# First DFT stage of batches 3 to 7: from one product over 94 rows to GpSimd sums and differences of mirrored rows and two products over 120 rows

## The chip, the cores and the metric

The kernel runs on one NeuronCore of a Trainium2 chip. Its engines have queues of their own and meet at semaphores: TensorE (PE, matmul), VectorE (DVE), ScalarE (ACT), GpSimd (POOL) and SyncE (SP, which here only issues DMAs). GpSimd issues DMAs too, in the same queue as its arithmetic, one instruction after the other. The metric is the time of one execution on the device in microseconds; the median of the runs of the kernel before is 788.53 us.

## The reference, cut to what matters

```python
# x (8, 3008, 256), filt_r and filt_i (1505, 256), w_in (256, 2048), w_out (2048, 256), alpha (2048)
X = np.fft.rfft(x, axis=1)
y = np.fft.irfft(X * (filt_r + 1j * filt_i), n=3008, axis=1)      # global filter along the sequence
h = y.reshape(24064, 256) @ w_in
g = h + np.sin(alpha * h) ** 2 / alpha
out = g @ w_out                                                   # float32
```

The two dense products with the snake activation between them are most of the arithmetic. The change touches only the first step of the forward transform.

## The kernel before, in words

The length 3008 is 47 * 64. A row n of a batch is 64 * n1 + n2, with n1 from 0 to 46 and n2 from 0 to 63. The transform of one batch (class `Spectral`) has four stages:

- `first` (L178, product in L181): a DFT of length 47 over n1, for 24 frequencies s, real and imaginary part. An x tile holds 94 partitions (47 n1, and for each the two halves of n2) and 8 columns n2 of 256 channels. One product of 94x96 weights with 512 columns makes two of these 8. There are 16 products for each batch. `evac` (L155 to L162) copies each result from PSUM to the tile `t1_h` in fp16, in turn two on ACT (L160) and one on DVE (L162). After every fourth, one DMA on SP writes 8 columns to a buffer `d1` in DRAM (L186).
- `load_t2` (L193): eight DMAs on POOL read `d1` back with n2 on the partitions.
- `forward`, `product`, `cross`, `inverse` (u from 0 to 11): a DFT over n2 on PE (L201), a copy on ACT (L204), a swap of its halves by DMA (L208), three DVE operations of two SBUF operands each (`product` L215, `cross` L221 and L222) that multiply with the filter, and the inverse product on PE (L232).
- `load_t4` and `last`: back through DRAM, and the inverse over n1 into the tile `y` (L254).

The dense part works on chunks of 512 columns of `y`. `hidden` (L540) makes one of 16 blocks of 128 hidden units with two products into one of 4 PSUM buffers (pool `hps`). ACT computes a cosine of it (L544), and a DVE SCALAR_TENSOR_TENSOR reads the cosine from SBUF and the block from PSUM and writes `v` (L545). The PSUM buffer is free when this DVE operation is done. `project` (L557) makes the output from the `v` of the chunk before.

The order is written by hand. A loop counts steps, eight to a chunk: a step issues two `hidden`, one or two pieces of transform work from a sorted list, a part of `project`, and more transform work. `put(at, ...)` gives each piece the step where it is due. Batch b has z = 48 * b, and its pieces are due relative to z, so the transform of batch b runs beside the dense part of the batches before. Work of PE is let out at one piece for each half step, other work when it is due. This sets the order of each engine's queue; when an instruction runs depends on that order and on its semaphores alone. For batches 3 to 7 the dues were: x loads at z - 92 + 7 * ch, the 16 `first` at z - 67 + 0.66 * i, `load_t2` at z - 56, `forward` at z - 46.8 + 2.3 * u, `product` 1.5 and `cross` 4.5 later, `inverse` at z - 40.8 + 2.3 * u. An x load (L141) also waits for the latest L545 that was issued before it, so it starts close to its due step.

Of the kernel before, what the change touches and what calls it, by code (L numbers as in the profile page):

```python
# [9 lines left out]
FP16 = mybir.dt.float16  # L10
FP32 = mybir.dt.float32
BF16 = mybir.dt.bfloat16
UINT32 = mybir.dt.uint32
AFT = mybir.ActivationFunctionType
ALU = mybir.AluOpType
# [3 lines left out]
B, S, C = 8, 3008, 256  # L19
DFF = 2048  # L20
N1, N2 = 47, 64
NS, NQ = 24, 64
NR = 2 * N1
NK = 4 * NS
FUSED = 1


def dft_tables():

    n1, n2 = np.arange(N1), np.arange(N2)  # L30
    s, q = np.arange(NS), np.arange(NQ)
    ph = 2 * np.pi * np.outer(n1, s) / N1
    w = np.stack([np.cos(ph), -np.sin(ph)], 1)
    wf = np.zeros((N1, 2, 2, NS, 2))
    wi = np.zeros((2, NS, 2, N1, 2))
    v = np.stack([2 * np.cos(ph), -2 * np.sin(ph)], 0)
    v[0, :, 0], v[1, :, 0] = 1.0, 0.0
    for h in range(2):
        wf[:, h, :, :, h] = w
        wi[:, :, h, :, h] = v.transpose(0, 2, 1) * (8.0 / S)  # L40

    kap = np.where(q[:, None] < 32, s + N1 * q[:, None], s + N1 * (95 - q[:, None]))
    sg = np.where(q < 32, 1.0, -1.0)[:, None]
    th = 2 * np.pi * n2[:, None, None] * kap / S
    c, sn = np.cos(th), np.sin(th)
    d = np.zeros((2, N2, NS, 2, NQ))
    d[0, :, :, 0] = c.transpose(0, 2, 1)
    d[1, :, :, 0] = sn.transpose(0, 2, 1)
    d[0, :, :, 1] = (-sn * sg).transpose(0, 2, 1)
    d[1, :, :, 1] = (c * sg).transpose(0, 2, 1)  # L50
    f16 = np.float16
    wf, wi = wf.reshape(N1 * 2, 2, NS, 2), 2 * wi.reshape(2, NS, 2, NR)
    wf0, wi0 = np.zeros((96, 2, 2, 32)), np.zeros((2, 2, 32, NR))
    wf0[:NR, :, :, :NS] = wf.transpose(0, 1, 3, 2)
    wi0[:, :, :NS] = wi.transpose(0, 2, 1, 3)
    d = d.reshape(128, NS, 128).astype(f16)
    e = d.transpose(2, 1, 0) * f16(0.125)
    return (wf.reshape(NR, NK).astype(f16), wi.reshape(NK, NR).astype(f16), d,
            wf0.reshape(96, 128).astype(f16), wi0.reshape(128, NR).astype(f16), e)


# [1 line left out]
def kernel(  # L63
# [8 lines left out]
    out: bass.AP,  # L72
):
    nc = tc.nc
    wf_host, wi_host, d_host, wf0_host, wi0_host, e_host = dft_tables()
    wf_dram = nc.inline_tensor(wf_host, name="wf_tbl")
    wi_dram = nc.inline_tensor(wi_host, name="wi_tbl")
    d_dram = nc.inline_tensor(d_host, name="d_tbl")
    wf0_dram = nc.inline_tensor(wf0_host, name="wf0_tbl")
    wi0_dram = nc.inline_tensor(wi0_host, name="wi0_tbl")  # L80
# [6 lines left out]
    def after(ins, other):  # L87

        tc.add_manual_dep(ins.ins, other.ins.name, mybir.DependencyInfo(
            mybir.DependencyClass.Sync, mybir.DependencyReason.DATA), reason="order of loads")  # L90

    def pool(name, bufs, space=None):
        kw = {} if space is None else {"space": space}
        return ctx.enter_context(tc.tile_pool(name=name, bufs=bufs, **kw))

    cpool = pool("consts", 1)
    xpool = pool("xp", 4)
    t2pool = pool("t2", 4)
    xfpool = pool("xf", 3)
    ppool = pool("pp", 4)  # L100
# [4 lines left out]
    dpool = pool("dram", 2, DRAM)  # L105
    fps = pool("fps", 2, PSUM)
# [1 line left out]
    ops = pool("ops", 2, PSUM)  # L108

    wf_t = cpool.tile([NR, NK], FP16)  # L110
    t1_h = [cpool.tile([128, 16, C], FP16, name=f"t1_h{i}") for i in range(2)]
    t4_a = cpool.tile([128, 2, 16, C], FP16)
    t4_h = [t4_a[:, i] for i in range(2)]

    def by_half(t):

        return t.rearrange("p a (b c) -> p (a b) c", c=128)

    cos_all = cpool.tile([128, 4, 512], FP32)
    y = cpool.tile([128, 2, 2, 32, NR], FP16)  # L120
# [4 lines left out]
    for h in range(2):  # L125
        nc.sync.dma_start(out=x32[:, 4 * C * h:4 * C * h + 4 * C],
                          in_=bass.AP(tensor=x.tensor, offset=x.offset + 4 * h * C, ap=[[32 * C, 96], [1, 4 * C]]))
# [8 lines left out]
    marks = {}  # L136

    def load_x(b, ch):
        xt = xpool.tile([NR, 8, C], FP16, name=f"x_{b}_{ch}", tag="x")
        for n0, n in [(0, 8)] if b or ch < 3 else [(0, 4), (4, 4)]:  # L140
            ins = nc.gpsimd.dma_start(  # L141
                out=xt[:, n0:n0 + n],
                in_=bass.AP(tensor=x.tensor, offset=x.offset + (b * S + ch * 8 + n0) * C,
                            ap=[[32 * C, NR], [C, n], [1, C]]),
            )
        if b == 0:
            marks["x", ch] = ins
        if b == 1:
            marks["x1", ch] = ins
            after(ins, marks["w_out"])  # L150
        if b > 1:
            after(ins, marks["snake"])
        return xt
# [3 lines left out]
    def evac(dst, src, on_act=None):  # L157
        flip[0] = (flip[0] + 1) % 3
        if flip[0] if on_act is None else on_act:
            marks["act"] = nc.scalar.copy(out=dst, in_=src)  # L160
        else:
            marks["dve"] = nc.vector.tensor_copy(out=dst, in_=src)  # L162

    class Spectral:

        def __init__(self, b):
            self.b = b
            self.d1 = dpool.tile([2 * NS, N2, C], FP16, name=f"d1_{b}", tag="d1")
            self.d2 = dpool.tile([2 * NS, N2, C], FP16, name=f"d2_{b}", tag="d2")
            self.d1_rows = self.d1.rearrange("a (h n) c -> (a h) n c", h=2)  # L170
            self.d2_rows = self.d2.rearrange("a (h n) c -> (a h) n c", h=2)
            self.x, self.t2, self.t4, self.xf, self.xs, self.p = {}, {}, {}, {}, {}, {}
            self.fused = b >= FUSED

        def load_x(self, ch):
# [2 lines left out]
        def first(self, i):  # L178
            ch, j = divmod(i, 4)
            ps = fps.tile([128, 512], FP32, name=f"pa_{self.b}_{i}", tag="f")  # L180
            marks["pe"] = nc.tensor.matmul(out=ps[0:NK, :], lhsT=wf_t, rhs=self.x[ch][:, 2 * j:2 * j + 2, :],  # L181
                                           start=True, stop=True)
            r0 = 8 * (ch % 2)
            evac(t1_h[ch // 2][0:NK, r0 + 2 * j:r0 + 2 * j + 2, :], ps[0:NK, :])
            if j == 3:
                nc.sync.dma_start(out=self.d1_rows[:, 8 * ch:8 * ch + 8, :],   # L186
                                  in_=t1_h[ch // 2][0:NK, r0:r0 + 8, :])

        def load_t2(self, g):
            self.t2[g] = t2pool.tile([128, 6, C], FP16, name=f"t2_{self.b}_{g}", tag="t2")  # L190
# [73 lines left out]
    id32 = cpool.tile([16, 16], FP32)  # L264
    nc.scalar.dma_start(out=id32, in_=id32_dram.ap())

    x0 = [xpool.tile([NR, 8, C], FP16, name="x_0_0", tag="x")] + [load_x(0, ch) for ch in range(1, 4)]
    nc.gpsimd.dma_start(out=d_t, in_=d_dram.ap())
    id16 = cpool.tile([128, 128], FP16)
    nc.gpsimd.dma_start(out=id16, in_=id16_dram.ap())  # L270
# [25 lines left out]
    for g in range(2):  # L296
        gs = slice(12 * g, 12 * g + 12)
        for k, filt in enumerate((filt_r, filt_i)):
            for q in range(2):
                if (g, k, q) == (0, 1, 1):  # L300
# [3 lines left out]
                    out=f_t[k][64 * k + 32 * q:64 * k + 32 * q + 32, gs, :],  # L304
# [132 lines left out]

    def product_0(i):
        hc, w = blocks[i]
        p0[i] = xpool.tile([128, 2, 4, 128], FP16, name=f"p_0_{i}", tag="x")  # L440
        marks["products"] = nc.vector.tensor_tensor(
            out=p0[i].rearrange("p f s (k c) -> p f s k c", k=2),
            in0=xf0[i].rearrange("p s (k c) -> p s k c", k=2)[:, None].to_broadcast([128, 2, 4, 2, 64]),
            in1=filt_t[:, :, 4 * w:4 * w + 4].rearrange("p f s (k c) -> p f s k c", k=2)[..., 64 * hc:64 * hc + 64],
            op=ALU.mult)
# [24 lines left out]
            after(ins, marks["filt", 1, 1])  # L470
    nc.sync.dma_start(out=wf_t, in_=wf_dram.ap())
    nc.sync.dma_start(out=wi_t, in_=wi_dram.ap())
    w_out32 = vpool.tile([128, 16, C], FP32, name="w_out32", tag="v")
    for jb in range(0, 16, 8):
        ins = nc.sync.dma_start(out=w_out32[:, jb:jb + 8],
# [117 lines left out]
    def put(at, fn, *args, pe=False):  # L593
        pending.append((at, len(pending), pe, fn, args))
# [14 lines left out]
    for b in range(1, B):  # L609
        s = s1 if b == 1 else Spectral(b)  # L610
        z = 48 * b
        if b > 1:
            for ch in range(4):
                put((22,27,32,37)[ch] if b == 2 else z - 92 + 7 * ch, s.load_x, ch)
        for i in range(16):
            put(7.9 + 0.3 * i if b == 1 else 36 + 0.66 * i if b == 2 else z - 67 + 0.66 * i, s.first, i, pe=True)
        for g in range(4):
            put(12.5 if b == 1 else max(z - 56, 46.5), s.load_t2, g)
        for u in range(12):
            inv = 23.5 + 1.25 * u if b == 1 else 59 + 2.1 * u if b == 2 else z - 40.8 + 2.3 * u  # L620
            fwd = inv - (6 if b == 1 else 6)
            put(fwd, s.forward, u, pe=True)
            put(fwd + (0.5 if b == 1 else 1.5), s.product, u)
            if s.fused:
                put(fwd + (4 if b == 1 else 4.5), s.cross, u)
            put(inv, s.inverse, u, pe=True)
        for ch in range(4):
            put(z - (9.5 if b == 1 and ch < 3 else (10.5, 10.5, 10.5, 3)[ch]), s.load_t4, ch)
        for u in range(16):
            put(z + (u - (5 if b == 1 else 6.5) if u < 4 else 2 * u - 9), s.last, u, pe=True)  # L630
# [59 lines left out]
```

## Time and profile before

| | |
|---|---|
| runs before | 787.25, 788.53, 788.79 us; median 788.53 us |
| profiled execution, first to last instruction (span) | 786.7 us |
| median of the runs less that span | 1.8 us |
| PE / DVE / ACT / POOL busy | 773.5 / 657.6 / 616.5 / 79.5 us |
| granted TensorE clock | 1.000 |
| L181, the first-stage products of batches 1 to 7 | 112 |
| L215, L221, L222, the filter's DVE operations | 84 each |
| x loads on POOL, L141: POOL time of one, time to landing | 0.54 us, 4.9 us |
| loads of `d1`, L193: POOL time of one, time to landing | 0.67 us, 4.6 us |

The profile has no time of its own for the profiled execution beyond the span; the 1.8 us are what the runs show around it. Busy time of PE is the union of its matmuls. Because they overlap in the pipeline, the mean of one (0.38 us for 512 columns) is longer than what one adds to the end. The chain of work that ended last shows what each added.

### The profile page before, as it was taken

The page shows a single profiled execution, that of the slowest core. Times are in us where ns is not written, and L with a number is a line of the kernel's source. Part 1 is how long each engine was busy: PE and PEld are TensorE (multiplying, and loading weights), DVE is VectorE, ACT ScalarE, POOL GpSimd, SP SyncE. Part 2 cuts the span into 40 slices and gives each one's busy share as a digit, 9 for nine tenths or more (in the row PEclk, how much of TensorE's full clock was granted, in tenths as well). Part 3 has the DMA queues.
Part 4 walks back from the last instruction along what each step waited for, and adds up shares of the span by engine and source line. Part 5 has one row for each costly group of instructions (what it writes and reads, how often), then busy time and mean ns, then how long its engine had stood idle before and what let it go on. Part 6 is the DMA issues. An engine that isn't in the chain of part 4 may idle for free.

```text
span 786.7 us, 16619 instructions
## 1 busy us (share of the span) xinstructions
PE 773.5 (98%) x5799; PEld 535.0 (68%) x5799; DVE 657.6 (84%) x1172; ACT 616.5 (78%) x1208; POOL 79.5 (10%) x125
## 2 busy tenths in 40 slices
PE   8998999999999999999999999999999999999998
PEld 4756766666667766777666766777666776766666
DVE  7887997899878997799977998799987999777773
ACT  5797878888878887888877888788887887777674
POOL 6442000200020000200020000200002000000000
PEclk9999999999999999999999999999999999999999
DMA  9965568665473646554575454845556243421111
GB/s 213 258 131 157 113 145 223 153 123 133 134 198 84 134 99 195 143 120 110 120 200 128 103 106 139 224 87 113 129 155 181 61 99 81 117 62 28 41 41 54
DMA packets 87692, 100.99 MB, mean 128 GB/s; under 512 B 14488, under 2 KB 75944, under 8 KB 87608
## 3 DMA queue, kind: packets, MB, share of 16 engines
q1 hardware_dynamic: 78032, 73.73, 34.5%
q0 software_dynamic: 9360, 26.15, 17.7%
q8 instruction: 45, 0.74, 0.4%
q14 instruction: 39, 0.32, 0.1%
q10 hardware_dynamic: 216, 0.05, 0.0%
HBM read 55.72 MB, written 46.66 MB: 130 GB/s over the span
## 4 chain that ended last, share of the span: by engine, by line
PE 89%; DVE 5%; ACT 2%; DMA 2%; issue 1%; SPq 1%; ACTq 0%; DVEq 0%
PE po L557 39%; PE ph L540 38%; PE pa L181 3%; PE pd L254 2%; DVE v L545 2%; PE pb L201 2%; PE pc L232 2%; DMA xs<-xf 1%; ACT cos_all L544 1%; DMA al<-in_moe_alpha_dram 1%; PE warm L381 1%; PE pc L453 0%; SPq L585 0%; ACT t_h L160 0%; DVE filt_t L162 0%
## 5 line engine op out<-in xcount | busy, mean ns | idle before, releaser
L545 DVE SCALAR_TENSOR_TENSOR v<-cos_all,ph 128x512 f16<-128x512 f32 (+1 forms) x768 | 483.0, 672 | 108.1 <-ACT cos_all L544 104.8
L544 ACT ACTIVATE cos_all<-ph 128x512 f32<-128x512 f32 (+1 forms) x768 | 411.1, 592 | 93.9 <-PE ph L540 92.9
L540 PE MATMUL ph<-y,w 128*128 128x512 f16 (+1 forms) x1536 | 388.4, 374 | 1.7 <-DVE y L162 0.9
L557 PE MATMUL po<-w,v 128*128 128x256 f16 x3008 | 389.5, 272 | 0.0
L557 PEld LDWEIGHTS <-v 128*128 128x128 f16 x3008 | 288.3, 98 | 77.7 <-issue 1.4
L540 PEld LDWEIGHTS <-w 128*128 128x128 f16 x1536 | 147.9, 98 | 106.5 <-issue 6.1
L565 ACT COPY o<-po 128x512 f32<-128x512 f32 (+1 forms) x97 | 55.6, 574 | 20.2 <-PE po L557 12.9
L204 ACT CAST xf<-pb 128x512 f16<-128x512 f32 x84 | 50.0, 595 | 16.4 <-PE pb L201 12.7
L193 POOL DMA_DIRECT2D t<-d x56 | 36.4, 669 | 204.6 <-DMA out_dram<-o 99.8
L160 ACT CAST t_h<-pa 96x512 f16<-96x512 f32 x74 | 43.3, 585 | 10.6 <-PE pa L181 10.5
L141 POOL DMA_DIRECT2D x<-in_x_dram x32 | 17.1, 536 | 298.2 <-PE pc L232 171.2
L160 ACT CAST y<-pd 128x376 f16<-128x376 f32 (+1 forms) x82 | 39.5, 482 | 8.8 <-PE pd L254 5.3
L254 PEld LDWEIGHTS <-t_a 96*128 96x128 f16 x448 | 31.3, 97 | 18.7 <-issue 0.4
L181 PE MATMUL pa<-x,wf_t 94*96 94x512 f16 x112 | 42.3, 381 | 1.6 <-ACT t_h L160 1.3
L160 ACT CAST g<-pc 128x512 f16<-128x512 f32 x58 | 34.4, 593 | 8.0 <-PE pc L232 7.7
L222 DVE TENSOR_TENSOR p<-p,xs 128x512 f16<-128x512 f16 x84 | 35.7, 425 | 2.9
L254 PE MATMUL pd<-wi_t,t_a 96*128 96x94 f16 x448 | 37.1, 204 | 0.0
L221 DVE TENSOR_TENSOR xs<-xs,filt_t 128x512 f16<-128x512 f16 x84 | 35.2, 420 | 0.8 <-DMA xs<-xf 0.8
L215 DVE TENSOR_TENSOR p<-xf,filt_t 128x512 f16<-128x512 f16 x84 | 35.2, 419 | 0.0
L232 PE MATMUL pc<-p,e_t 128*128 128x256 f16 x168 | 32.1, 273 | 0.8 <-ACT xf L204 0.5
L201 PE MATMUL pb<-t,d_t 128*128 128x256 f16 x168 | 32.1, 272 | 0.2
L162 DVE CAST y<-pd 128x376 f16<-128x376 f32 (+2 forms) x46 | 24.9, 544 | 1.5 <-PE pd L343 1.0
(66 smaller groups left out, 264.4 us busy)
## 6 DMA issues: line engine op xcount, KB each, us to landing
x<-in_x_dram POOLq DMA_DIRECT2D x30, 376.0 KB, 4.9
d<-t_h SPq DMA_DIRECT2D x28, 384.0 KB
t<-d POOLq DMA_DIRECT2D x56, 192.0 KB, 4.6
xs<-xf SPq DMA_DIRECT2D x168, 64.0 KB
d<-g SPq DMA_DIRECT2D x56, 192.0 KB
t_a<-d SPq DMA_DIRECT2D x28, 384.0 KB
out_dram<-o SPq DMA_DIRECT2D x104, 80.0 KB
w_out<-in_moe_w_out_dram SPq DMA_DIRECT2D x2, 1024.0 KB
```

The lines of the kernel that those rows point to most:

```text
L160: marks["act"] = nc.scalar.copy(out=dst, in_=src)
L181: marks["pe"] = nc.tensor.matmul(out=ps[0:NK, :], lhsT=wf_t, rhs=self.x[ch][:, 2 * j:2 * j + 2, :], start=True, stop=True)
L193: nc.gpsimd.dma_start(out=self.t2[g][64 * p:64 * p + 64, :, :], in_=self.d1[a0:a0 + 6, :, :].rearrange("s n c -> n s c"))
L201: nc.tensor.matmul(out=ps[:, i, :], lhsT=d_t[:, s, :], rhs=self.t2[s // 6][:, s % 6, :], start=True, stop=True)
L204: nc.scalar.copy(out=self.xf[u], in_=ps)
L232: nc.tensor.matmul(out=ps[:, i, :], lhsT=e_t[:, 2 * w + i, :], rhs=pt[:, i, :], start=(k == 0), stop=(k == len(pr) - 1))
L254: nc.tensor.matmul(out=psv[:, i, :], rhs=wi_t, start=True, stop=True, lhsT=t4_h[ch // 2][0:NK, n0 % 16 + i, cb * 128:cb * 128 + 128])
L540: nc.tensor.matmul(out=ps[:, 0:n], lhsT=w1[:, cb, jb * 128:jb * 128 + 128], rhs=y_cols[:, cb, c0:c0 + n], start=(cb == 0), stop=(cb == 1))
L544: nc.scalar.activation(out=cs[:, 0:n], in_=ps[:, 0:n], func=AFT.Sin, bias=float(np.pi / 2))
L545: marks["snake"] = nc.vector.scalar_tensor_tensor(out=v[k][:, jb, 0:n], in0=cs[:, 0:n], scalar=-1.0, in1=ps[:, 0:n], op0=ALU.add, op1=ALU. ...
L557: nc.tensor.matmul(out=pso[k][:, t % 2, :], lhsT=v[k][:, jb, 128 * t:128 * t + 128], rhs=w2[:, jb, :], start=(jb == 0), stop=(jb == 15))
L565: nc.scalar.copy(out=o[:, i0:t % 2 + 1, :], in_=pso[k][:, i0:t % 2 + 1, :])
```

## The change

For a real input, the cosine is even and the sine odd in n1, so rows n1 and 47 - n1 can be added and subtracted first. Batches 3 to 7 (`FOLDED = 3`) do this on GpSimd:

- A batch's 64 columns n2, and one of padding ahead of them, are cut into 5 groups (j) of 13 (l). `mirror[0]` holds the rows n1 = 1 to 23 for the 5 groups on 115 partitions, and the five groups of row 0 on 5 more; `mirror[1]` holds rows 46 down to 24, and zeros on the last 5 (cleared once, `start_folding`). They lie in the four x slots, which are now one tile `x_all`.
- `load_mirror` loads pairs of columns l: 14 DMAs and one for row 0, in place of 4, all on POOL. They are due at z - 92 to z - 75.1.
- `fold(i)`, i from 0 to 6: one GpSimd addition of 120x512 into one of 4 small buffers `sums`, and one subtraction in place (120x256 for i = 6). In POOL's queue they come after the batch's loads and ahead of its `load_t2`.
- `first_folded(i, k)`: one product of 120x120 with 512 columns for the sums (k = 0, real part) and one for the differences (k = 1, imaginary part); with 256 columns for i = 6. 14 products and 13 copies in place of 16 and 16.
- `d1` is written by two pairs of DMAs on SP, after i = 3 and i = 6. `load_t2` is due at z - 53 instead of z - 56.

A table `wp_t` is loaded at the start, on SP, ahead of `w_out`. Batches 0 to 2 compute as before.

```diff
-    xpool = pool("xp", 4)
-    t1_h = [cpool.tile([128, 16, C], FP16, name=f"t1_h{i}") for i in range(2)]
+    t1_a = cpool.tile([128, 2, 16, C], FP16)
+    t1_h = [t1_a[:, i] for i in range(2)]
+    wp_t = cpool.tile([NF, 2, NF], FP16)
+    x_all = cpool.tile([128, 4, 8, C], FP16)
...
+    STORES = {3: 0, 6: 8}
+    NP = (NL + 1) // 2
+    x_rows = x_all.rearrange("p a n c -> p (a n) c")
+    mirror = [x_rows[:, 16 * k:16 * k + NL, :] for k in range(2)]
+    sums = [t[0:NF, NL:NL + 2, :] for t in (t1_h[0], t1_h[1], x_rows[:, 0:16], x_rows[:, 16:32])]
+
+    def start_folding():
+        nc.gpsimd.memset(mirror[1].bitcast(UINT32), 0)
...
+        def load_mirror(self, k, l0, n):
+            rows = [mirror[k][0:NF - NJ, l0:l0 + n]] + ([] if k or l0 else [mirror[k][NF - NJ:NF]])
+            for at, t in zip((N2 * (N1 - 1) if k else N2, 0), rows):
+                run = n if at else NL
+                ins = nc.gpsimd.dma_start(
+                    out=t, in_=bass.AP(tensor=x.tensor, offset=x.offset + (self.b * S + at - 1 + l0) * C,
+                                       ap=[[NL * C, NJ], [-N2 * C if k else N2 * C, NS - 1 if at else 1],
+                                           [1, run * C]]))
+                after(ins, marks["snake"])
+
+        def fold(self, i):
+            l0, n = 2 * i, min(2, NL - 2 * i)
+            xa, xb = [t[0:NF, l0:l0 + n, :] for t in mirror]
+            self.e[i] = sums[i % 4]
+            nc.gpsimd.tensor_tensor(out=self.e[i][:, 0:n, :], in0=xa, in1=xb, op=ALU.add)
+            nc.gpsimd.tensor_tensor(out=xa, in0=xa, in1=xb, op=ALU.subtract)
+
+        def first_folded(self, i, k):
...
+            nc.tensor.matmul(out=dst, lhsT=wp_t[:, k, :], rhs=src, start=True, stop=True)
+            if n == 2:
+                evac(t1_a[0:NF, k, l0:l0 + 2, :], ps[0:NF])
+            elif k == 1:
+                evac(t1_a[0:NF, :, l0, :], ps[0:NF])
+            if i in STORES and k == 1:
+                lo = STORES[i]
+                n = l0 + n - lo
+                for part in range(2):
+                    nc.sync.dma_start(out=self.d1_fold[part, :, lo:lo + n, :], in_=t1_a[0:NF, part, lo:lo + n, :])
...
-        if b > 1:
-            for ch in range(4):
-                put((22,27,32,37)[ch] if b == 2 else z - 92 + 7 * ch, s.load_x, ch)
-        for i in range(16):
-            put(7.9 + 0.3 * i if b == 1 else 36 + 0.66 * i if b == 2 else z - 67 + 0.66 * i, s.first, i, pe=True)
+        if s.folded:
+            if b == FOLDED:
+                put(z - 94, start_folding)
+            for i in range(NP):
+                for k in range(2):
+                    put(z - 92 + 2.6 * i + 1.3 * k, s.load_mirror, k, 2 * i, min(2, NL - 2 * i))
+            for i in range(NP):
+                at = z - 64 + 1.4 * i
+                put(at - 3.4, s.fold, i)
+                for k in range(2):
+                    put(at + 0.7 * k, s.first_folded, i, k, pe=True)
...
         for g in range(4):
-            put(12.5 if b == 1 else max(z - 56, 46.5), s.load_t2, g)
+            put(12.5 if b == 1 else 46.5 if b == 2 else z - 53, s.load_t2, g)
```

More of the change, by code (lines that the diff above doesn't have):

```diff
@@ L25 @@
 FUSED = 1
+FOLDED = 3
+NJ, NL = 5, 13
+NF = NJ * NS
 def dft_tables():
@@ L57, in dft_tables @@
     e = d.transpose(2, 1, 0) * f16(0.125)
-    return (wf.reshape(NR, NK).astype(f16), wi.reshape(NK, NR).astype(f16), d,
+    even = np.cos(ph[:NS])
+    odd = -np.sin(ph[:NS])
+    wp = np.einsum("kis,jm->jiksm", np.stack([even, odd]), np.eye(NJ))
+    wp = np.concatenate([wp[:, 1:].reshape(NF - NJ, 2, NF), wp[:, 0].reshape(NJ, 2, NF)])
+    return (wp.astype(f16), wf.reshape(NR, NK).astype(f16), wi.reshape(NK, NR).astype(f16), d,
             wf0.reshape(96, 128).astype(f16), wi0.reshape(128, NR).astype(f16), e)
@@ L74 @@
     nc = tc.nc
-    wf_host, wi_host, d_host, wf0_host, wi0_host, e_host = dft_tables()
+    wp_host, wf_host, wi_host, d_host, wf0_host, wi0_host, e_host = dft_tables()
     wf_dram = nc.inline_tensor(wf_host, name="wf_tbl")
     wi_dram = nc.inline_tensor(wi_host, name="wi_tbl")
+    wp_dram = nc.inline_tensor(wp_host, name="wp_tbl")
     d_dram = nc.inline_tensor(d_host, name="d_tbl")
@@ L117, in by_half, with x_tile @@
         return t.rearrange("p a (b c) -> p (a b) c", c=128)
+    x_all = cpool.tile([128, 4, 8, C], FP16)
+    x_made = []
+    def x_tile():
+        x_made.append(x_all[:, len(x_made) % 4])
+        return x_made[-1]
     cos_all = cpool.tile([128, 4, 512], FP32)
@@ L138, in load_x @@
     def load_x(b, ch):
-        xt = xpool.tile([NR, 8, C], FP16, name=f"x_{b}_{ch}", tag="x")
+        xt = x_tile()[0:NR]
         for n0, n in [(0, 8)] if b or ch < 3 else [(0, 4), (4, 4)]:
@@ L167, in __init__ @@
             self.b = b
-            self.d1 = dpool.tile([2 * NS, N2, C], FP16, name=f"d1_{b}", tag="d1")
+            self.folded = b >= FOLDED
+            if self.folded:
+                self.d1_all = dpool.tile([2 * NS, NJ * NL, C], FP16, name=f"d1_{b}", tag="d1f")
+                self.d1 = self.d1_all[:, 1:1 + N2, :]
+                self.d1_fold = self.d1_all.rearrange("(k s) (j l) c -> k (s j) l c", k=2, j=NJ)
+            else:
+                self.d1 = dpool.tile([2 * NS, N2, C], FP16, name=f"d1_{b}", tag="d1")
+                self.d1_rows = self.d1.rearrange("a (h n) c -> (a h) n c", h=2)
             self.d2 = dpool.tile([2 * NS, N2, C], FP16, name=f"d2_{b}", tag="d2")
-            self.d1_rows = self.d1.rearrange("a (h n) c -> (a h) n c", h=2)
             self.d2_rows = self.d2.rearrange("a (h n) c -> (a h) n c", h=2)
-            self.x, self.t2, self.t4, self.xf, self.xs, self.p = {}, {}, {}, {}, {}, {}
+            self.e, self.x, self.t2, self.t4, self.xf, self.xs, self.p = {}, {}, {}, {}, {}, {}, {}
             self.fused = b >= FUSED
@@ L187, in first @@
                                   in_=t1_h[ch // 2][0:NK, r0:r0 + 8, :])
+        def load_mirror(self, k, l0, n):
[14 more added lines that the diff above has]
+        def first_folded(self, i, k):
+            l0, n = 2 * i, min(2, NL - 2 * i)
+            if n == 2 or k == 0:
+                self.ps1 = fps.tile([128, 2, C], FP32, name=f"pa_{self.b}_{i}_{k}", tag="f")
+            ps = self.ps1
+            if k == 0:
+                src = self.e[i][:, 0:n, :]
+            else:
+                src = mirror[0][0:NF, l0:l0 + n, :]
+            dst = ps[0:NF, 0:2, :] if n == 2 else ps[0:NF, k:k + 1, :]
+            nc.tensor.matmul(out=dst, lhsT=wp_t[:, k, :], rhs=src, start=True, stop=True)
[8 more added lines that the diff above has]
+                    nc.sync.dma_start(out=self.d1_fold[part, :, lo:lo + n, :], in_=t1_a[0:NF, part, lo:lo + n, :])
         def load_t2(self, g):
@@ L265 @@
     nc.scalar.dma_start(out=id32, in_=id32_dram.ap())
-    x0 = [xpool.tile([NR, 8, C], FP16, name="x_0_0", tag="x")] + [load_x(0, ch) for ch in range(1, 4)]
+    x0 = [x_tile()[0:NR]] + [load_x(0, ch) for ch in range(1, 4)]
     nc.gpsimd.dma_start(out=d_t, in_=d_dram.ap())
@@ L439, in product_0 @@
         hc, w = blocks[i]
-        p0[i] = xpool.tile([128, 2, 4, 128], FP16, name=f"p_0_{i}", tag="x")
+        p0[i] = x_tile()[:, 0:4].rearrange("p n (f c) -> p (n f) c", f=2).rearrange("p (f s) c -> p f s c", f=2)
         marks["products"] = nc.vector.tensor_tensor(
@@ L472 @@
     nc.sync.dma_start(out=wi_t, in_=wi_dram.ap())
+    nc.sync.dma_start(out=wp_t, in_=wp_dram.ap())
     w_out32 = vpool.tile([128, 16, C], FP32, name="w_out32", tag="v")
@@ L611 @@
         z = 48 * b
-        if b > 1:
-            for ch in range(4):
-                put((22,27,32,37)[ch] if b == 2 else z - 92 + 7 * ch, s.load_x, ch)
-        for i in range(16):
-            put(7.9 + 0.3 * i if b == 1 else 36 + 0.66 * i if b == 2 else z - 67 + 0.66 * i, s.first, i, pe=True)
+        if s.folded:
[9 more added lines that the diff above has]
+                    put(at + 0.7 * k, s.first_folded, i, k, pe=True)
+        else:
+            if b > 1:
+                for ch in range(4):
+                    put((22, 27, 32, 37)[ch], s.load_x, ch)
+            for i in range(16):
+                put(7.9 + 0.3 * i if b == 1 else 36 + 0.66 * i, s.first, i, pe=True)
         for g in range(4):
-            put(12.5 if b == 1 else max(z - 56, 46.5), s.load_t2, g)
+            put(12.5 if b == 1 else 46.5 if b == 2 else z - 53, s.load_t2, g)
         for u in range(12):
```

## The prediction

> **What bounds the kernel now.** I read the page first (shares of the engines), then the busy times in windows, then the chain that ended last, then the groups by shape, and last the timeline where the change puts its GpSimd work.
>
> ```profile
> span 786.7 us, 16619 instructions
> ...
> PE 773.5 (98%) x5799; PEld 535.0 (68%) x5799; DVE 657.6 (84%) x1172; ACT 616.5 (78%) x1208; POOL 79.5 (10%) x125
> ```
>
> ```profile
> core 0: us, PE busy (x) PEld busy (x) DVE busy (x) ACT busy (x) POOL busy (x), PEclk, DMA share, GB/s
> ...
> 178.00:191.00 13.00, 13.00 (x95) 9.07 (x94) 12.47 (x25) 10.92 (x22) 0.51 (x1) 1.00 0.55 117
> ...
> 274.00:287.00 13.00, 13.00 (x95) 9.20 (x94) 11.89 (x23) 10.96 (x21) 0.51 (x1) 1.00 0.54 114
> ...
> 366.00:379.00 13.00, 13.00 (x95) 9.07 (x94) 12.14 (x24) 10.60 (x22) 0.51 (x1) 1.00 0.53 118
> ```
>
> ```profile
> 400.45 0.22 PE pa L181
> 400.67 0.88 PE po L557 x8
> 401.55 0.86 PE ph L540 x4
> ```
>
> ```profile
> L545 DVE SCALAR_TENSOR_TENSOR v<-cos_all,ph 128x512 f16<-128x512 f32 x704 | 450.4, 683 | 93.0 <-ACT cos_all L544 89.9
> ...
> L215 DVE TENSOR_TENSOR p<-xf,filt_t 128x512 f16<-128x512 f16 x84 | 35.2, 419 | 0.0
> ...
> L482 POOL TENSOR_TENSOR w<-w_in,y 128x512 f16<-128x512 f32 x2 | 2.6, 1280 | 0.0
> ```
>
> PE has no gap at a full clock: 13.00 of 13.00 us in each window. In the chain a product of 512 columns adds 0.215 us (0.86 for 4) and one of 256 columns 0.109 us (0.88 for 8). So columns taken from PE count fully, as long as nothing stops it. What could is DVE: it averages 84%, but in these windows (the second half of a batch's filter stage) it is at 91 to 96% (11.89 to 12.47 of 13). POOL is all but idle, so its own time is no bound.
>
> The timeline of batch 3's filter stage, where the change lets GpSimd work for batch 4:
>
> ```profile
> 275.13 1.03 PE L540 MATMUL ph<-y,w 128*128 128x512 f16 x4
> ...
> 275.70 0.42 DVE L221 TENSOR_TENSOR xs<-xs,filt_t 128x512 f16<-128x512 f16 x1
> ...
> 276.15 0.42 DVE L222 TENSOR_TENSOR p<-p,xs 128x512 f16<-128x512 f16 x1
> 276.49 1.28 DVE L545 SCALAR_TENSOR_TENSOR v<-cos_all,ph 128x512 f16<-128x512 f32 x2
> ...
> 277.09 1.03 PE L540 MATMUL ph<-y,w 128*128 128x512 f16 x4
> 277.69 0.69 DVE L162 CAST g<-pc 128x512 f16<-128x512 f32 x1
> ...
> 278.29 0.42 DVE L215 TENSOR_TENSOR p<-xf,filt_t 128x512 f16<-128x512 f16 x1
> 278.62 1.28 DVE L545 SCALAR_TENSOR_TENSOR v<-cos_all,ph 128x512 f16<-128x512 f32 x2
> ...
> 279.05 1.03 PE L540 MATMUL ph<-y,w 128*128 128x512 f16 x4
> ...
> 279.81 0.42 DVE L221 TENSOR_TENSOR xs<-xs,filt_t 128x512 f16<-128x512 f16 x1
> ...
> 280.27 0.42 DVE L222 TENSOR_TENSOR p<-p,xs 128x512 f16<-128x512 f16 x1
> 280.61 1.28 DVE L545 SCALAR_TENSOR_TENSOR v<-cos_all,ph 128x512 f16<-128x512 f32 x2
> 280.78 1.03 PE L540 MATMUL ph<-y,w 128*128 128x512 f16 x4
> ```
>
> The slack that PE has against a late DVE is read here. The four products at 275.13 fill two of the four hidden buffers; DVE frees the first at 277.1 (half of the pair that starts at 276.49), and PE writes it again at 279.05: 1.9 us to spare. For the next pair it is 279.3 against 280.78: 1.5 us. I take 1.7 us. DVE may run that late; beyond it, each microsecond stops PE.
>
> **The products.** Before, a batch has 16 * 0.215 = 3.44 us; after, 12 * 0.215 + 2 * 0.109 = 2.80 us. Saved: 0.65 us a batch, 3.2 us for five. All of it lies on the chain.
>
> **Copies out of PSUM.** 13 in place of 16 a batch: about two of 0.585 us less on ACT (L160) and one of 0.68 us on DVE (L162). Both lie beside PE, and after the filter stage; counted at nothing.
>
> **Loads.** 15 issues in place of 4 a batch. At 0.54 us (the x row; the loads of `d1` take 0.67) this is 8.1 instead of 2.1 us of POOL, which sits idle about 13 us ahead of each x load now. The last load is due at z - 75.1, the first product at z - 64. A step is 1.96 us (the x loads at 268.68 and 282.42 are 7 steps apart), so 22 us cover a landing of 4.9 (9.5 for the slowest x load of the trace). Bytes are the same. The memset of 1664 words runs once, in POOL's idle time; `wp_t`, 58 KB on SP, delays `w_out` by some 0.3 us at the 200 GB/s of the start, and POOL is busy with L482 until 40 us in any case.
>
> **The folds, as POOL work.** 12 operations of 1.28 us (L482, 128x512) and two of half the length, some 0.74 us by the slope to the 768 form (1.82 us): 17 us a batch. Nothing in POOL's queue holds folds 0 to 3 to their due step (z - 67.4): they wait for the loads only, so they start as soon as the last load is issued, at z - 75.1. Fold 4 reuses a buffer of `sums` and waits for product 0 at z - 64; it has 11 us until product 4. Behind them POOL holds only `load_t2`. So PE does not wait for a fold unless an operation takes about three times its row.
>
> **The folds beside DVE.** z - 75.1 of batch 4 is 274.4 us in this trace, so eight GpSimd operations run from 275.0 for 10 us and more, among the filter's DVE operations. This meeting is not in the trace: L482 and L514 run from 30.5 to 47.5 us, after the last DVE operation with two SBUF operands. The bounds: beside L514, the L545 operations (one operand in SBUF, one in PSUM) kept their 683 ns, so the low end is no effect. The high end is that each DVE operation of two SBUF operands waits for a whole GpSimd one, 1.28 us. L215 reads two streams at 1.2 elements per ns, against one SBUF stream at 0.75 for L545, so L545's rows say little for it; as the nearest thing I take it that the two exclude each other and whoever comes first goes first. The walk along the timeline, with 1.28 us for a fold operation: the DVE operations of 275.70, 276.15, 278.29, 279.81, 280.27 and 283.24 wait 0.58, 1.25, 0.88, 0.18, 1.24 and 0.20 us, each wait moving the later ones: 4.3 us, less 0.15 of idle time. With 1.05 us (the 1024 form of L514, 1.91 us, less a start of 0.2, halved) they come to 2.65. Middle: 3.4 us. Less the slack of 1.7, PE stops for 1.7 us; the same stage with the same due steps stands in each of the five batches: 8.5 us. Ends: 0, and (8 * 1.28 - 1.7) * 5 = 43 us.
>
> The rule that bears on this is in the Trainium skill, "SBUF — State Buffer", section "Who interferes with whom": a DVE instruction with at most one SBUF input outside the two-port modes does not contend with GpSimd, which this trace's 683 ns beside L514 agrees with; one with two SBUF inputs contends with a GpSimd instruction that reads SBUF, and the second to come is blocked for the whole of the first. No row here shows the latter. By the rule the sum is the walk's; without it, the first rival's.
>
> **`d1` and `load_t2`.** The last product moves from z - 57.1 to z - 54.9; `forward` stays. In batch 4 now: last first-stage product 308.89, its store issued on SP at 310.29, first `load_t2` at 315.66, first `forward` at 325.80. With the same distances: 1.4 + 5.4, 0.3 for the second store of the pair, 0.67 until the second load of the first tile, 4.6 to land: 12.4 us. PE has, in the changed order, 12.7 us of work (columns at the chain's rate) between the two in batches 4 and 6, 14.8 in the others. The first three `load_t4` of the batch before stand between the store pairs on SP and wait for neither long. I take 0.3 us each in batches 4 and 6, 0.6 in all; ends: 0, and with the slowest landing of the trace (8.4) 2 * 3.5 + 3 * 1.4 = 11 us.
>
> **Sum.** 786.7 - 3.2 + 8.5 + 0.6 = 792.6 us of span. The median stands 1.8 us above the span, so 794.4 us, 5.9 above 788.53. A difference under 0.2% (1.6 us) could not be told from none.
>
> **Rivals.**
> 1. The meeting on DVE costs nothing, or less than the 1.7 us that the buffers absorb. Then 788.53 - 3.2 + 0.6 = 785.9, or 785.3 with no late `load_t2`. It decides where the six waits average under 0.28 us. For it: L545 and L514 side by side, and PE that never waits now. Against it: DVE at 91 to 96% just there, with cross's two operations back to back, so the second meets a fold that was waiting.
> 2. The exclusion is real but short: 0.3 to 1 us of PE a batch, 1.5 to 5 in all: 787 to 791.
> 3. `load_t2` lands late in most batches: up to 11 - 3.2, 796.3, with DVE undisturbed. Against it: the median landing just fits.
> 4. The columns saved don't shorten the chain (PE would then show new waits of its own): 788.5. Against it: 100% busy PE at a clock of 1.00.
>
> **How the numbers follow.** Forecast (PE stopped for 1 us or more in each filter stage): 0.57, 790.9 and up; its upper part, two more whole waits a batch, would pass 803. Rival 1: 0.28, of which 0.03 ends within 0.2%. Rival 2: 0.09, of which 0.07 within. Rival 3: 0.04, slower. Rival 4: 0.02, same. Faster 0.25, same 0.12, slower 0.63. The range leaves out a tenth above, and a little below: 785.2 to 803. The forecast alone: 790.5 to 804.
>
> **What would show it.** Right: L215, L221 or L222 with a mean well over 0.42 us, or unexplained gaps ahead of them, in the stages from z - 75 to z - 69; new waits PE <- DVE v of 1 to 3 us there; ten first-stage products fewer in all (32 + 70 in place of 112), at 0.22 us on the chain. Wrong: those three rows at 420 to 425 ns still and PE at 13.00 of 13.00; fold operations far from 1.0 to 1.3 us; or waits PE <- DMA ahead of L201's line.

## The result and the profile after

The change makes the kernel slower: a median of 799.61 us (797.59 to 802.87) against 788.13 us (787.25 to 788.79) on the same chip, a ratio of 1.0148 with a 95% interval of 1.0131 to 1.0164. The profiled execution of after is the fastest of its runs: it took 797.59 us and spans 795.8 us, 9.1 us more than before's span. The slower runs of after span up to 801.1 us, at granted clocks of 0.993 to 0.998; that part of the median is not in the trace that is read here.

First the page of after, total and engines:

```profile
span 795.8 us, 16797 instructions
...
PE 771.4 (97%) x5789; PEld 532.6 (67%) x5789; DVE 672.1 (84%) x1167; ACT 613.2 (77%) x1198; POOL 197.8 (25%) x251
```

PE works 2.1 us less than before (773.5), and the span is 9.1 us longer: PE idles 24.4 us, where it idled 13.2. The groups by line say beside whom. The columns are busy time and mean ns of one, then idle time ahead of them and what ended it:

```profile
L293 DVE TENSOR_TENSOR p<-p,xs 128x512 f16<-128x512 f16 x84 | 44.0, 524 | 2.9
...
L303 PE MATMUL pc<-p,e_t 128*128 128x256 f16 x168 | 32.2, 273 | 12.3 <-DVE p L293 11.5
L292 DVE TENSOR_TENSOR xs<-xs,filt_t 128x512 f16<-128x512 f16 x84 | 40.7, 484 | 0.7 <-DMA xs<-xf 0.7
L286 DVE TENSOR_TENSOR p<-xf,filt_t 128x512 f16<-128x512 f16 x84 | 40.4, 481 | 0.0
L236 POOL TENSOR_TENSOR t_a<-x_all 120x512 f16<-120x512 f16 x20 | 24.9, 1246 | 60.6 <-PE pa L249 60.5
```

The same in the kernel before (L215, with a mean of 419 ns, is shown in the prediction):

```profile
L222 DVE TENSOR_TENSOR p<-p,xs 128x512 f16<-128x512 f16 x84 | 35.7, 425 | 2.9
L221 DVE TENSOR_TENSOR xs<-xs,filt_t 128x512 f16<-128x512 f16 x84 | 35.2, 420 | 0.8 <-DMA xs<-xf 0.8
...
L232 PE MATMUL pc<-p,e_t 128*128 128x256 f16 x168 | 32.1, 273 | 0.8 <-ACT xf L204 0.5 <-DVE p L222 0.2
```

And the wait of PE in after (in total, times, longest):

```profile
PE pc L303 <- DVE p L293: 11.5, 12, 2.7
```

The three DVE operations of the filter (L215, L221 and L222 of before, where they took 419, 420 and 425 ns in the mean) are 19.0 us longer in sum: 125.1 against 106.1, 3.8 us for each of the five batches. The inverse product, L303, waits 11.5 us for the last of them, which it did for 0.2 us before. This one wait, twelve times up to 2.7 us, is the lost time. In windows of ten microseconds around the folds of batch 4, the second batch that is folded:

```profile
core 0: us, PE busy (x) PEld busy (x) DVE busy (x) ACT busy (x) POOL busy (x), PEclk, DMA share, GB/s
...
267.00:277.00 10.00, 10.00 (x78) 6.98 (x77) 9.29 (x19) 8.43 (x17) 3.69 (x5) 1.00 0.76 136
277.00:287.00 10.00, 8.16 (x57) 5.31 (x56) 9.93 (x15) 6.42 (x12) 8.74 (x7) 1.00 0.31 74
287.00:297.00 10.00, 10.00 (x71) 6.83 (x70) 9.82 (x20) 7.76 (x16) 0.17 (x1) 1.00 0.32 80
297.00:307.00 10.00, 10.00 (x67) 6.50 (x66) 7.74 (x13) 8.40 (x17) 6.03 (x6) 1.00 0.32 83
```

PE loses 1.84 us in the second window, where POOL is at 8.74 of 10 and DVE at 9.93. In the last one POOL runs the other folds (6.03 us) and PE loses nothing: the filter's DVE operations are over by then. The timeline of the second window (start, duration) shows the meeting one by one:

```profile
281.76 1.04 PE L629 MATMUL po<-w,v 128*128 128x256 f16 x8
...
282.28 1.15 POOL L237 TENSOR_TENSOR x_all<-x_all 120x512 f16<-120x512 f16 x1
282.30 1.41 DVE L292 TENSOR_TENSOR xs<-xs,filt_t 128x512 f16<-128x512 f16 x1
282.63 1.02 PE L612 MATMUL ph<-y,w 128*128 128x512 f16 x4
...
283.39 1.33 POOL L236 TENSOR_TENSOR x_all<-x_all 120x512 f16<-120x512 f16 x1
283.75 1.26 DVE L293 TENSOR_TENSOR p<-p,xs 128x512 f16<-128x512 f16 x1
284.80 1.22 POOL L237 TENSOR_TENSOR x_all<-x_all 120x512 f16<-120x512 f16 x1
284.93 2.47 DVE L617 SCALAR_TENSOR_TENSOR v<-cos_all,ph 128x512 f16<-128x512 f32 x4
285.06 0.39 PE L303 MATMUL pc<-p,e_t 128*128 128x256 f16 x2 [1.41 <-DVE p L293]
```

L292 starts 0.02 us behind a GpSimd subtraction, which ends at 283.43; L292 ends at 283.71, 0.28 us later. L293 starts while the addition of 283.39 runs, and ends 0.29 us after it (285.01 against 284.72). So an operation that takes 0.42 us alone lasts until 0.28 us after the GpSimd operation's end: it reads as begun, held until then, and done at once after it. The hold is no wait in the profile: it lies inside the DVE instruction's duration. GpSimd pays too: an addition or subtraction that starts while such a DVE operation is still running takes up to 1.33 us, where 1.15 is its time alone. L617, with one operand in SBUF, is not held (2.47 for four). Then PE stands for 1.41 us at L303.

### The profile page after: what moved, and what is told of

The parts are those of the page before. It is cut to its first block, busy times and chain, and to the rows that moved or that the text cites. A ratio compares the mean times of both kernels' runs of the same rounds, so it can differ in the third digit from the quotient of the medians.

```text
span 795.8 us, 16797 instructions
## 1 busy us (share of the span) xinstructions
PE 771.4 (97%) x5789; PEld 532.6 (67%) x5789; DVE 672.1 (84%) x1167; ACT 613.2 (77%) x1198; POOL 197.8 (25%) x251
## 4 chain that ended last, share of the span: by engine, by line
PE 80%; DVE 12%; ACT 2%; DMA 2%; issue 2%; SPq 1%; POOL 0%; ACTq 0%; DVEq 0%; POOLq 0%
PE po L629 36%; PE ph L612 34%; DVE v L617 5%; PE pd L325 2%; PE pc L303 2%; PE pb L272 2%; DVE p L293 2%; PE pa L249 2%; DVE xs L292 1%; ACT cos_all L616 1%; DMA x_all<-in_x_dram 1%; DMA out_dram<-o 1%; PE pa L214 1%; DVE p L286 1%; SPq L657 1%
## 5 line engine op out<-in xcount | busy, mean ns | idle before, releaser
L617 DVE SCALAR_TENSOR_TENSOR v<-cos_all,ph 128x512 f16<-128x512 f32 (+1 forms) x768 | 482.0, 671 | 103.7 <-ACT cos_all L616 101.3
L226 POOL DMA_DIRECT2D x_all<-in_x_dram x75 | 47.4, 634 | 160.0 <-DVE v L617 159.4
L293 DVE TENSOR_TENSOR p<-p,xs 128x512 f16<-128x512 f16 x84 | 44.0, 524 | 2.9
L177 ACT CAST t_a<-pa 120x512 f16<-120x512 f32 (+1 forms) x65 | 38.4, 590 | 10.3 <-PE pa L249 5.7
L303 PE MATMUL pc<-p,e_t 128*128 128x256 f16 x168 | 32.2, 273 | 12.3 <-DVE p L293 11.5
L292 DVE TENSOR_TENSOR xs<-xs,filt_t 128x512 f16<-128x512 f16 x84 | 40.7, 484 | 0.7 <-DMA xs<-xf 0.7
L286 DVE TENSOR_TENSOR p<-xf,filt_t 128x512 f16<-128x512 f16 x84 | 40.4, 481 | 0.0
L236 POOL TENSOR_TENSOR t_a<-x_all 120x512 f16<-120x512 f16 x20 | 24.9, 1246 | 60.6 <-PE pa L249 60.5
L237 POOL TENSOR_TENSOR x_all<-x_all 120x512 f16<-120x512 f16 (+1 forms) x35 | 39.0, 1116 | 2.7
```

The source lines that it names most:

```text
L286: marks["prod", u] = nc.vector.tensor_tensor(out=pt, in0=self.xf[u], in1=f_t[k][:, 2 * u:2 * u + 2, :], op=ALU.mult)
L292: nc.vector.tensor_tensor(out=xs, in0=xs, in1=f_t[1][:, 2 * u:2 * u + 2, :], op=ALU.mult)
L293: nc.vector.tensor_tensor(out=p, in0=p, in1=xs, op=ALU.add)
L303: nc.tensor.matmul(out=ps[:, i, :], lhsT=e_t[:, 2 * w + i, :], rhs=pt[:, i, :], start=(k == 0), stop=(k == len(pr) - 1))
L617: marks["snake"] = nc.vector.scalar_tensor_tensor(out=v[k][:, jb, 0:n], in0=cs[:, 0:n], scalar=-1.0, in1=ps[:, 0:n], op0=ALU.add, op1=ALU. ...
```

## The experiments

**The folds held back, first form.** Edit of after (`after(ins, other)` makes `ins` wait for `other`):

```diff
-            nc.gpsimd.tensor_tensor(out=self.e[i][:, 0:n, :], in0=xa, in1=xb, op=ALU.add)
+            ins = nc.gpsimd.tensor_tensor(out=self.e[i][:, 0:n, :], in0=xa, in1=xb, op=ALU.add)
+            if i == 0:
+                after(ins, marks["cross"])
...
-            nc.vector.tensor_tensor(out=p, in0=p, in1=xs, op=ALU.add)
+            marks["cross"] = nc.vector.tensor_tensor(out=p, in0=p, in1=xs, op=ALU.add)
...
-                at = z - 64 + 1.4 * i
-                put(at - 3.4, s.fold, i)
+                start = z - (63.3 if b == FOLDED else 64.9)
+                put(start + 0.01 * i, s.fold, i)
                 for k in range(2):
-                    put(at + 0.7 * k, s.first_folded, i, k, pe=True)
+                    put(start + 2.0 + 1.25 * i + 0.62 * k, s.first_folded, i, k, pe=True)
```

> The change, with its folds held until the last cross of the batch before has run, so that no GpSimd addition meets a DVE operation of two SBUF operands; the products follow at 1.25 steps a pair. Theory (the two exclude each other, PE then waits for cross): L286, L292 and L295 back to a mean of 0.42 us from 0.48 to 0.52, the waits of PE for them (11.5 us) gone, and the 3.2 us of saved columns show: 784 to 786.5 us, a ratio to before of 0.995 to 0.998. Rival (loads, queues or the later load_t2 cost the time): those parts are still there, so 796 us or more.

Measured: 840.73 us, a ratio of 1.0653 (1.0633 to 1.0673). This missed, and by an error in the edit: all seven folds stood in the program ahead of the first product, so folds 4 to 6 reused buffers whose sums had yet to be read, and the first product of each batch waited for them (PE waited 43.1 us in five waits for the line of the additions). Its time says nothing on the question. Its rows do: the three DVE groups are back at 419 to 425 ns, and the inverse waits 0.2 us for them.

**The same, with each fold in its turn.** One line differs from the edit above:

```diff
-                put(start + 0.01 * i, s.fold, i)
+                put(start + 1.25 * i, s.fold, i)
```

> As the first run with folds held until the last cross, with each fold issued at 1.25 steps after the one before, so that the four buffers of sums are used in turn (there, all seven folds stood ahead of the first product and the last three overwrote buffers that products had yet to read; its time says nothing on the question). Theory (exclusion, PE waits for cross): the three DVE groups back to 0.42 us, no waits of PE for them, 784 to 787 us, 0.995 to 0.998 of before. Rival (loads, stores or products cost the time): 796 us or more.

Measured: 786.48 us against 788.93, a ratio of 0.9967 (0.9955 to 0.9979). It is faster than both kernels, than the one before by 0.3%. Its groups by line (the last one is the additions, now held):

```profile
L295 DVE TENSOR_TENSOR p<-p,xs 128x512 f16<-128x512 f16 x84 | 35.7, 425 | 2.9
L294 DVE TENSOR_TENSOR xs<-xs,filt_t 128x512 f16<-128x512 f16 x84 | 35.1, 418 | 0.4 <-DMA xs<-xf 0.3
L288 DVE TENSOR_TENSOR p<-xf,filt_t 128x512 f16<-128x512 f16 x84 | 35.1, 417 | 0.0
...
L305 PE MATMUL pc<-p,e_t 128*128 128x256 f16 x168 | 32.1, 273 | 0.8 <-ACT xf L277 0.4 <-DVE p L295 0.2
...
L236 POOL TENSOR_TENSOR t_a<-x_all 120x512 f16<-120x512 f16 x20 | 23.0, 1152 | 100.3 <-DVE p L295 77.4 <-ACT cos_all L618 22.9
```

The three rows are back at 0.42 us, the inverse waits for them 0.2 us in all, and an addition takes 1.15 us. The loads, the stores, the 14 products, the folds and the late `load_t2` are all still there, so none of these costs the time; when the folds run does.

**The additions alone, in the kernel before.** Edit of before:

```diff
+    def beside(i):
+        ja, jb, js, jd = d_t[0:120, 0:4], d_t[0:120, 4:8], t1_h[0][0:120, 2 * i:2 * i + 2], t1_h[1][0:120, 2 * i:2 * i + 2]
+        js, jd = [t.rearrange("p n (h c) -> p (n h) c", h=2) for t in (js, jd)]
+        ins = nc.gpsimd.tensor_tensor(out=js, in0=ja, in1=jb, op=ALU.add)
+        if i == 0:
+            after(ins, marks["snake"])
+        nc.gpsimd.tensor_tensor(out=jd, in0=js, in1=jb, op=ALU.subtract)
...
+        if b > 2:
+            for i in range(4):
+                put(z - 75.1 + 0.01 * i, beside, i)
```

> The kernel before, with nothing of the change but eight GpSimd operations of 120x512 fp16 for each of batches 3 to 7 at the place where the change's folds 0 to 3 ran, on tables and a tile that is idle there; their results are not used. Theory: the three DVE groups of the filter get 3 to 4 us a batch longer, and PE idles 2 to 2.5 us a batch: 798 to 802 us. Rival (the cost comes with the loads, the stores or the products): no change, 787 to 789 us.

Measured: 802.15 us, a ratio of 1.0164 (1.0149 to 1.0179). The groups by line:

```profile
L222 DVE TENSOR_TENSOR p<-p,xs 128x512 f16<-128x512 f16 x84 | 42.4, 504 | 2.9
...
L221 DVE TENSOR_TENSOR xs<-xs,filt_t 128x512 f16<-128x512 f16 x84 | 42.3, 503 | 1.6 <-DMA xs<-xf 1.5
L215 DVE TENSOR_TENSOR p<-xf,filt_t 128x512 f16<-128x512 f16 x84 | 39.9, 475 | 0.0
...
L232 PE MATMUL pc<-p,e_t 128*128 128x256 f16 x168 | 32.2, 273 | 12.7 <-DVE p L222 11.1 <-DVE g L162 1.4
```

40 GpSimd operations whose results nobody uses make the kernel before slower by 13 us, through the same wait: DVE 18.5 us longer in these rows (124.6 against 106.1), PE 11.1 us in front of the inverse. This is the disputed cost by itself. It lies 0.15 us above the range that was expected.

**Memsets and copies in the same place.** Edits of `beside`: two memsets of 1280 words for each i, or two copies of 120x1024 fp16.

```diff
+            ins = nc.gpsimd.memset(t1_h[k][:, 0:10].bitcast(UINT32), 0)
```

> As the run with eight additions, but with eight GpSimd memsets of 1280 words, which write SBUF and read nothing, for about the same time. If the two engines meet on reading: DVE rows stay at 0.42 us and the time at 787 to 789 us. If they meet on writing, or GpSimd work of any kind holds DVE: 796 to 802 us.

```diff
+            ins = nc.gpsimd.tensor_copy(out=t1_h[k][0:120, 0:4].rearrange("p n (h c) -> p (n h) c", h=2),
+                                        in_=d_t[0:120, 8 * k:8 * k + 8])
```

> The kernel before with eight GpSimd copies of 120x1024 fp16 (one SBUF input) for each of batches 3 to 7, at the place of the eight additions. If any GpSimd read of SBUF excludes a DVE operation of two SBUF operands: L215, L221 and L222 above 0.45 us in the mean, and a time of 795 us or more if the copies take about 1 us each. If only two-input GpSimd operations do: rows at 0.42 us and 787 to 790 us.

Measured: 789.33 us with memsets, a ratio of 1.0001 (0.9991 to 1.0010); 797.11 us with copies, which ran only once, against 788.93. Groups of the kernel with memsets, then of the one with copies:

```profile
L612 POOL MEMSET t_h<- 128x1280 uint32 x40 | 44.5, 1163 | 23.7 <-DVE v L545 23.7
...
L222 DVE TENSOR_TENSOR p<-p,xs 128x512 f16<-128x512 f16 x84 | 35.7, 425 | 2.9
L221 DVE TENSOR_TENSOR xs<-xs,filt_t 128x512 f16<-128x512 f16 x84 | 35.2, 419 | 1.5 <-DMA xs<-xf 1.5
L215 DVE TENSOR_TENSOR p<-xf,filt_t 128x512 f16<-128x512 f16 x84 | 35.2, 419 | 0.0
```

```profile
L612 POOL COPY t_h<-d_t 120x1024 f16<-120x1024 f16 x40 | 43.8, 1142 | 23.6 <-DVE v L545 23.6
...
L222 DVE TENSOR_TENSOR p<-p,xs 128x512 f16<-128x512 f16 x84 | 41.4, 493 | 2.9
...
L221 DVE TENSOR_TENSOR xs<-xs,filt_t 128x512 f16<-128x512 f16 x84 | 39.1, 466 | 1.8 <-DMA xs<-xf 1.8
L215 DVE TENSOR_TENSOR p<-xf,filt_t 128x512 f16<-128x512 f16 x84 | 38.0, 452 | 0.0
```

A GpSimd operation that only writes holds nothing, for 44.5 us of it. One that reads a single operand does: the time comes from a single run, but the rows of its profile are clear, 452 to 493 ns where they had 419 to 425. So the two engines meet on reading. This is the rule of the Trainium skill, "SBUF — State Buffer", section "Who interferes with whom", which the prediction set beside the walk: a DVE operation of two SBUF inputs meets a GpSimd instruction that reads SBUF, and not one that only writes it. The additions and copies measure the first half, the memsets the second.

**No folds.** Edit of after: the two GpSimd operations of `fold` are left out, and the sums product reads `mirror[1]` as it was loaded.

> The change without its GpSimd additions and subtractions: the products take the raw mirrored rows, so the first stage of batches 3 to 7 is left incomplete. Everything else (loads, 14 products, stores, due steps) is the change's. It measures the saved columns and what the rest costs. Theory: 788.9 - 3.2 = 785.7 us, within 1 us either way. Rival (the rest is not free): above 788.

Measured: 784.86 us, a ratio of 0.9950 (0.9935 to 0.9965). The rest of the change saves 4.1 us by the medians, at the upper end of what was expected (3.2, within 1), and costs nothing that shows; the three DVE rows are at 418 to 425 ns, so the 75 loads that GpSimd issues in place of 20 do not hold DVE. The held folds come 1.6 us above it, which the two intervals just allow to be nothing.

**The inverse later.** Edit of after:

```diff
-            put(inv, s.inverse, u, pe=True)
+            put(inv + (1.5 if b > 1 else 0), s.inverse, u, pe=True)
```

> The change, with each inverse product of batches 2 to 7 due 1.5 steps (2.9 us) later, so that it may wait longer for cross; folds and their meeting with DVE are untouched. If the inverse's place behind cross is all that stops PE: its waits for cross fall from 11.5 us to under 3, and the time to 790 to 793 us. If the slack of the hidden buffers (1.7 us of a DVE delay of 3.8 us a batch) stands right behind it, PE stops for about as long, at other lines (hidden, L612): 796 us or more.

Measured: 800.72 us, a ratio of 1.0149 (1.0133 to 1.0164), that of the change itself. The waits of PE, in order of length (in total, times, longest):

```profile
PE ph L612 <- DVE v L617: 9.1, 9, 1.5
PE pa L249 <- DVE t_a L179: 1.5, 1, 1.5
```

Given 2.9 us more, the inverse waits 0.2 us for `cross` where it waited 11.5, and PE stops for the hidden buffers instead: 9.1 us there, 10.6 with the line below. The inverse only stood first in a row of waits on a DVE that was late as a whole; the second form of this run's expectation holds.

**The folds on DVE.** Edit of after: `nc.gpsimd.tensor_tensor` becomes `nc.vector.tensor_tensor` in both lines of `fold`.

> The change, with the fold's additions and subtractions on DVE in its own order at their due step (z - 67.4 on). 14 operations at 0.42 us are 5.6 us a batch of DVE time, in a stretch where DVE is 72 to 90% busy. Theory: no exclusion, so 785 to 789 us, set by how much of the 5.6 us DVE has free. Rival (the rest of the change costs the time): 796 us or more.

Measured: 791.60 us, a ratio of 1.0045 (1.0029 to 1.0060). No exclusion, and the operations take 0.42 us in place of 1.15, but the time lies 3 us above before, where 785 to 789 was expected. At their due step the first folds lie among the last operations of the filter, where DVE has nothing free:

```profile
290.00:300.00 10.00, 8.95 (x63) 5.80 (x61) 9.83 (x21) 6.79 (x14) 0.00 (x0) 1.00 0.26 66
300.00:310.00 10.00, 10.00 (x66) 6.41 (x65) 9.73 (x21) 8.13 (x17) 0.00 (x0) 1.00 0.40 100
```

DVE is at 9.83 and 9.73 of 10, and PE loses 1.05 us in the first of the two; over all batches it waits 4.4 us for `cross`. Whether a later place would make DVE the better engine was not tried.

## Why the prediction was right, and where its sizes were off

The direction, the mechanism and the place in the schedule were right; the median came out 5 us above the forecast, and inside the range.

- **The products.** 3.2 us forecast. Without folds the medians differ by 4.1 us; with held folds PE is busy 3.5 us less (770.0 against 773.5). Right, where PE does not wait; in the change itself its busy time falls by only 2.1 us, and why it is 1.4 us above that of the held folds was not tested.
- **The folds as POOL work.** 1.28 us taken from L482's row; 1.15 alone and 1.33 to 1.34 with a DVE operation in the way. The issues of the loads took 0.63 us each where 0.54 was taken, with nothing waiting for them. The folds started where the due steps did not put them, as forecast: in after, the first fold of batch 4 starts at 275.79, 0.65 us after the last load's issue at 275.14. No product waited for a fold.
- **The folds beside DVE.** The walk gave 2.65 to 4.2 us of delay a batch (4.3 less 0.15 of idle time), and the middle, 3.4, was taken; measured 3.8 in the mean of the five. The choice of exclusion over coexistence was right, and the additions alone in the kernel before show it.
- **The slack** is the step that was read from the wrong wait; that its size was close is luck. The forecast put the stop at the hidden buffers (PE <- DVE v). It came at the inverse, which is due 1.5 steps behind `cross`. The hidden buffers are the next to stop PE, as the later inverse shows. Of 19.0 us of DVE delay PE lost 11.5 (2.3, 1.8, 1.9, 3.5 and 1.8 in the five batches), so 7.5 us or 1.5 a batch were absorbed, against 1.7 taken. The two small errors, 0.4 us of delay and 0.2 of slack for each batch, make the 3.0 us between 8.5 and 11.5.
- **`load_t2`.** 0.6 us forecast; PE has no wait for a DMA at `forward`'s line, though the median landing of the loads of `d1` was 6.0 us where 4.6 was taken. Wrong, and too small to matter. Rival 3 falls with it.
- **The sum.** 792.6 us of span forecast, 795.8 measured in the profiled execution. Three terms were off: 3.0 us more of waiting, as above; 1.1 us less saved on PE (2.1 instead of 3.2); and the 0.6 us at `forward` that did not come. That makes 3.5 us, near the 3.2 by which the span was missed; 0.2 us of the inverse's wait stood there before. The median lies 2.0 us above the profiled execution's own 797.59; the cause of that part was not tested.

Rivals 1 and 2 (no cost, or a short one) fall with the additions alone. Rival 4 falls too: the saved columns do shorten the chain, as soon as the folds are out of the way.

## What to carry to other kernels

An engine that is idle most of the time is not free to use: ask what it shares with the engine that is nearly full, and at which stage. As these runs show it, GpSimd work that reads SBUF belongs in a stretch where DVE runs no operation of two SBUF operands. Here a wait for the last `cross` put it there; the due step in the program's order had not, because nothing on GpSimd's queue held the folds back. A hold of this kind shows as a longer mean of an unchanged operation, so compare means per group before looking at waits.

## What the runs showed of the hardware that was not expected

A DVE operation of two SBUF operands (128x512 fp16, 0.42 us alone) that meets a GpSimd read ends 0.28 us after the GpSimd operation does. Because GpSimd operations stood back to back, it met one almost every time: in after, 22 of the 25 such operations beside the first eight fold operations of each batch were held. The longest, a `product` of 1.89 us, started 0.43 us ahead of the addition that held it; that does not fit the rule that whoever comes first goes first, and why is not shown. A GpSimd copy with a single operand of 1024 elements (1.14 us) holds DVE as well, with 12.4 us in the same three rows (118.5 against 106.1), where the two-operand additions made 18.5.
